# Staging of the cast weights, one bit step on ACT, and a new ranking of all operations in a hashed-attention and channel-mix kernel

## The chip, the core and the metric

The kernel runs on one core of a Trainium2 chip. The metric is the device time of one execution in microseconds. The core has five engines that work side by side: TensorE (PE, matmuls), VectorE (DVE), ScalarE (ACT), GpSimd (POOL), and SyncE (SP), which here only issues DMAs. Each engine takes its instructions in the order in which the program lists them, and an instruction that must wait holds up all that stand behind it on that engine.

## The reference

Attention of 4 batches with 8 heads each, 768 positions and head size 64, in which a query sees only the keys with the same 6 hash bits; its output, laid out as 768 x 512, goes through a channel mix with a squared-ReLU feed-forward and a sigmoid gate.

```
q_bits = (q @ proj > 0);  k_bits = (k @ proj > 0)            # 6 bits each
scores = where(bucket(q) == bucket(k), q @ k.T / 8, -1e9)
attn   = softmax(scores) @ v                                 # 4 x 8 x 768 x 64
x      = attn transposed to 4 x 768 x 512
xk = mu_k * x + (1 - mu_k) * x_prev;  xr = mu_r * x + (1 - mu_r) * x_prev
k  = max(xk @ w_k, 0)                                        # 512 -> 1024
out = sigmoid(xr @ w_r) * ((k * k) @ w_v)                    # 1024 -> 512
```

## The kernel before

The 32 heads are worked in 16 pairs (n = 0 to 15), four pairs to a batch. For a pair, q, k and v are loaded by SP (`nat`, `vn`; 384 KB each). DVE splits q and k into a high and a low fp16 part (`hi` L554 or L614, `lo` L557 or L619), DMA transposes them (`tr`, L561), or, for pairs 0 and 1, PE does (L632) and DVE or ACT copies the result out of PSUM (L637, L639). PE multiplies by the projection (L580, or L656 for pair 0), and DVE turns the signs into two values (`bx`, L583). Four small DMAs of 9 KB (`row`, L593) put these bits as extra rows beside the head dimensions, so that the score matmul (L696) adds a large constant for each bit that agrees; ACT's Exp (L700) with a bias then gives zero wherever a bit differs. For pair 0 the bits are written straight from PSUM, without the DMAs: by DVE (L664), or by ACT with a Sign function (L662). Which engine does which step is in the table `FIRST`, with the three entries split, copy out, bits. PE multiplies by v (L726), DVE divides (L742), the tile is transposed (PE at L752 for the first pairs and the last, else a DMA at L758), and the mixes `xk` and `xr` are formed on DVE. For v itself POOL makes column sums (L511 to L517) from which later pairs subtract the mean (L530, L536).

After four pairs, the batch's channel mix follows: `kp` (L816) with a ReLU on ACT (L820) and a square on DVE (L823) into the twelve tiles `k2`; `r` (L835) with a Tanh on ACT (L838); `v` (L845), and DVE's product (L852) into three tiles `os`, stored by SP. Its matmuls are mixed among those of later pairs' attention.

The weights come as fp32. w_k is converted by the DMA itself, issued from POOL. w_r (two loads, `wl4` and `wl5`) and w_v (four loads, `wl6` to `wl9`) are loaded by SP into an fp32 staging place, 512 KB each (L457), and cast on POOL (`wc4` to `wc9`, L464). Before, the first four stage in the memory of `k2` (L448), which the squares of batch 0 fill later, and the last two in a buffer `wst` of two places (L451).

The order on every engine is made by a planner written in the kernel (`Plan`, L108). Each operation is added with its engine, an assumed duration, what it reads and writes, and a rank. The planner goes through modelled time and lets each free engine take the ready operation with the lowest rank. The ranks are the list `WANT` (L44): its entry i belongs to the i-th operation added (L129). `port=1` marks an operation that the planner lets wait for the port that DVE and POOL share in its model. Loads wait while the modelled DMA queue is over 1.5 us deep (L228), apart from those marked as urgent at the start. The planner runs on the host, when the program is built; the chip sees the resulting order only.

`wl4` to `wc9` are entries 39 to 50 of the list, a load and its cast in turn; entries 51 to 58 are the loads q head 0, q head 1, k head 0, k head 1 and v of pair 0, and q, k and v of pair 1.

Of the kernel before, what the change touches and what calls it, by code (L numbers as in the profile page):

```python
# [9 lines left out]
FP32 = mybir.dt.float32  # L10
# [29 lines left out]
def R(kind, n):  # L40
# [4 lines left out]
    2, 6, 7, 11, 16, 52, 25, 29, 35, 10, 15, 8, 4, 24, 21, 28, 22, 18, 23, 13, 3, 20, 5, 27,  # L45
    14, 1, 32, 34, 36, 39, 40, 19, 51, 37, 48, 61, 76, 88, 102, 320, 346, 409, 435, 478, 500, 382, 412, 366,
    388, 290, 309, 0, 12, 9, 17, 89, 31, 26, 133, 38, 41, 45, 55, 33, 56, 46, 69, 58, 70, 42, 43, 44,
    53, 60, 71, 30, 57, 66, 75, 50, 54, 72, 65, 108, 94, 59, 68, 80, 86, 101, 111, 62, 77, 182, 109, 112,
    116, 123, 49, 78, 99, 92, 73, 63, 87, 98, 74, 64, 96, 85, 47, 67, 84, 93, 107, 95, 124, 115, 119, 113,
    83, 91, 79, 82, 100, 104, 90, 97, 129, 134, 122, 127, 125, 130, 118, 81, 117, 120, 140, 146, 150, 154, 156, 141,  # L50
    155, 159, 163, 165, 168, 172, 175, 177, 185, 180, 110, 103, 240, 148, 152, 158, 161, 106, 105, 126, 121, 114, 138, 162,
    167, 192, 179, 186, 174, 143, 145, 170, 223, 173, 224, 144, 151, 166, 169, 149, 157, 136, 142, 153, 164, 132, 139, 187,
    188, 193, 199, 207, 176, 178, 181, 184, 209, 214, 221, 237, 243, 259, 264, 171, 210, 302, 203, 212, 219, 227, 135, 137,
    147, 128, 131, 160, 183, 190, 215, 202, 226, 206, 233, 235, 230, 232, 249, 250, 211, 222, 218, 217, 200, 204, 197, 195,
    205, 208, 191, 196, 265, 267, 270, 273, 274, 236, 238, 244, 251, 253, 277, 281, 285, 292, 295, 301, 189, 198, 256, 257,
    263, 269, 272, 194, 201, 229, 234, 239, 248, 271, 276, 297, 293, 305, 286, 275, 278, 242, 241, 254, 260, 280, 283, 262,
    314, 282, 288, 245, 246, 258, 266, 225, 216, 289, 291, 294, 300, 306, 296, 298, 299, 307, 312, 317, 322, 325, 327, 331,
    337, 340, 367, 370, 372, 404, 411, 410, 424, 431, 347, 359, 363, 356, 374, 381, 436, 441, 447, 414, 440, 448, 462, 469,
    482, 379, 390, 452, 439, 461, 504, 490, 495, 510, 497, 503, 509, 446, 456, 513, 516, 522, 534, 508, 515, 535, 507, 518,
    531, 467, 472, 520, 547, 551, 586, 473, 480, 539, 556, 561, 609, 532, 555, 571, 583, 591, 619, 599, 608, 559, 587, 615,  # L60
    921, 594, 604, 616, 627, 633, 933, 611, 622, 641, 648, 658, 946, 220, 261, 349, 318, 323, 328, 336, 348, 343, 352, 213,
    228, 279, 231, 247, 268, 303, 308, 324, 316, 330, 345, 339, 351, 361, 377, 329, 338, 354, 360, 321, 332, 334, 344, 315,
    326, 310, 313, 311, 319, 417, 420, 421, 427, 437, 394, 397, 400, 403, 406, 353, 449, 474, 485, 492, 529, 496, 501, 358,
    416, 373, 333, 341, 342, 350, 357, 355, 362, 252, 255, 335, 284, 287, 304, 368, 375, 386, 402, 391, 399, 425, 433, 405,
    418, 376, 383, 401, 413, 384, 393, 387, 398, 457, 465, 392, 407, 364, 369, 451, 454, 455, 464, 499, 481, 487, 494, 512,
    514, 365, 588, 603, 606, 613, 628, 610, 620, 458, 443, 519, 371, 378, 380, 415, 432, 422, 426, 385, 389, 423, 444, 453,
    468, 502, 521, 533, 550, 538, 544, 428, 450, 483, 491, 505, 511, 429, 445, 471, 476, 543, 548, 486, 498, 523, 527, 477,
    484, 526, 528, 530, 537, 540, 552, 567, 577, 582, 593, 430, 602, 632, 634, 645, 649, 647, 652, 395, 489, 541, 396, 408,
    419, 434, 442, 438, 459, 479, 488, 524, 470, 475, 506, 546, 554, 564, 580, 563, 598, 656, 664, 605, 612, 569, 585, 653,
    657, 592, 601, 568, 573, 576, 579, 646, 650, 589, 597, 672, 674, 682, 694, 699, 659, 665, 666, 671, 676, 463, 709, 735,  # L70
    741, 752, 755, 749, 779, 805, 811, 831, 788, 806, 830, 766, 770, 783, 768, 773, 786, 838, 846, 850, 827, 833, 839, 778,
    787, 796, 781, 798, 803, 851, 863, 867, 845, 855, 860, 861, 871, 881, 795, 808, 818, 835, 875, 884, 916, 925, 930, 905,
    911, 915, 910, 918, 926, 815, 826, 931, 939, 942, 961, 880, 886, 923, 943, 949, 958, 902, 951, 948, 959, 963, 966, 978,
    984, 985, 991, 995, 1006, 1005, 1015, 1019, 1029, 1032, 1036, 996, 1004, 954, 974, 1011, 1021, 553, 595, 614, 536, 542, 545, 558,
    566, 572, 581, 460, 466, 493, 517, 525, 574, 635, 640, 654, 651, 663, 678, 661, 670, 683, 693, 679, 686, 607, 617, 621,
    626, 630, 637, 669, 675, 639, 644, 624, 629, 712, 715, 720, 725, 731, 687, 690, 700, 704, 706, 590, 780, 801, 804, 807,
    812, 810, 832, 549, 560, 660, 557, 562, 565, 668, 680, 673, 692, 578, 584, 623, 618, 625, 643, 721, 727, 747, 733, 751,
    739, 705, 714, 696, 702, 710, 719, 703, 707, 726, 728, 732, 742, 740, 748, 729, 734, 717, 723, 737, 743, 750, 756, 784,
    754, 759, 762, 767, 774, 697, 862, 889, 890, 906, 909, 896, 903, 636, 718, 822, 631, 638, 642, 677, 688, 684, 698, 570,
    575, 667, 596, 600, 695, 746, 760, 789, 797, 776, 771, 849, 858, 834, 840, 785, 791, 813, 820, 772, 792, 775, 782, 793,  # L80
    799, 761, 764, 753, 758, 870, 874, 888, 853, 899, 821, 823, 864, 868, 872, 701, 924, 945, 947, 955, 956, 953, 1016, 685,
    745, 852, 681, 689, 691, 708, 722, 713, 730, 655, 662, 724, 738, 744, 763, 800, 825, 856, 844, 837, 847, 857, 865, 895,
    913, 919, 929, 809, 814, 824, 829, 843, 848, 885, 892, 928, 934, 914, 920, 964, 968, 971, 976, 979, 952, 962, 967, 969,
    972, 736, 983, 994, 999, 1003, 1007, 1020, 1022, 1047, 1054, 1058, 1040, 1045, 1051, 1074, 1077, 1085, 1014, 1023, 1026, 1112, 1117, 1122,
    1123, 1126, 1131, 1110, 1116, 1119, 1057, 1065, 1071, 1145, 1151, 1154, 1133, 1140, 1144, 1115, 1124, 1127, 1063, 1076, 1078, 1163, 1169, 1173,
    1147, 1157, 1164, 1177, 1180, 1183, 1101, 1106, 1111, 1082, 1091, 1196, 1197, 1204, 1207, 1167, 1171, 1188, 1193, 1201, 1199, 1209, 1211, 1202,
    1217, 1222, 1227, 1214, 1218, 1148, 1205, 1220, 1223, 1221, 1226, 1236, 1241, 1246, 1249, 1229, 1233, 1224, 1232, 1238, 1242, 757, 794, 869,
    842, 854, 859, 970, 981, 977, 986, 711, 716, 828, 765, 769, 802, 866, 876, 887, 908, 894, 904, 1001, 1008, 993, 998, 1024,
    1027, 891, 897, 957, 960, 941, 944, 901, 907, 877, 882, 1012, 1018, 1031, 1033, 1035, 1038, 1041, 1050, 1052, 1056, 1060, 1064, 987,
    1070, 1087, 1089, 1094, 1100, 1097, 1102, 898, 817, 990, 873, 879, 883, 927, 932, 935, 938, 777, 790, 878, 816, 819, 912, 989,  # L90
    992, 997, 1000, 1010, 1017, 1044, 1048, 965, 980, 1025, 1030, 1061, 1067, 936, 975, 1068, 1073, 1028, 1034, 1107, 1113, 982, 988, 1081,
    1096, 1098, 1105, 1108, 1118, 1121, 1125, 1130, 1134, 940, 1136, 1149, 1150, 1152, 1156, 1159, 1162, 893, 900, 973, 1039, 1043, 1049, 1053,
    917, 922, 950, 836, 841, 937, 1075, 1080, 1099, 1103, 1093, 1086, 1155, 1160, 1104, 1109, 1161, 1165, 1083, 1084, 1037, 1059, 1114, 1120,
    1072, 1079, 1088, 1095, 1092, 1090, 1175, 1176, 1181, 1184, 1185, 1135, 1139, 1158, 1166, 1168, 1055, 1189, 1198, 1200, 1203, 1208, 1206, 1234,
    1002, 1009, 1013, 1042, 1046, 1062, 1066, 1179, 1182, 1170, 1174, 1141, 1146, 1190, 1192, 1129, 1132, 1138, 1142, 1172, 1178, 1128, 1137, 1143,
    1153, 1210, 1212, 1213, 1215, 1216, 1187, 1186, 1191, 1194, 1195, 1069, 1219, 1225, 1228, 1230, 1231, 1235, 1237, 1240, 1239, 1243, 1245, 1258,
    1263, 1265, 1244, 1248, 1251, 1253, 1257, 1259, 1250, 1254, 1256, 1264, 1269, 1271, 1255, 1260, 1262, 1261, 1266, 1268, 1285, 1289, 1291, 1270,
    1275, 1277, 1273, 1278, 1280, 1267, 1272, 1274, 1290, 1295, 1297, 1282, 1286, 1288, 1276, 1281, 1284, 1287, 1292, 1294, 1247, 1252, 1296, 1298,
# [189 lines left out]
def kernel(  # L288
# [52 lines left out]
    def buf(shape, dt, name):  # L341
        return pool.tile(shape, dt, name=name, tag=name)
# [569 lines left out]
```

## Time and profile before

| | us |
|---|---|
| median of 4 runs | 257.84 |
| lowest and highest | 257.11, 258.87 |
| the profiled execution, its own time | 258.16 |
| its span in the profile | 256.4 |
| ACT, the Exps of L700, 144 times | 140.7 |
| PE, scores of L696, 384 times | 82.1 |
| PE, last matmul ends | 252.6 |

The span is the time from the first to the last event of one execution as the profiler saw it; the execution's own time is 1.76 us longer. Busy times of PE overlap a little, because matmuls are pipelined. The granted PE clock is 0.99 in the mean.

### The profile page before, as it was taken

The numbers are of one execution on the slowest core, as the hardware profiler recorded it, in microseconds if no ns is written. First come the engines' busy times: TensorE is split into PE (matmuls) and PEld (weight loads), VectorE is DVE, ScalarE is ACT, GpSimd is POOL, SyncE is SP. The second block draws the span as 40 slices with busy tenths as digits, with TensorE's granted clock in tenths as the row PEclk, the third lists the DMA queues.
The fourth block names the chain that finished last, engine by engine and source line by source line (L and its number), as shares of the span: only waits on it lengthen the run. The fifth ranks groups of instructions, "written<-read, shape, count | busy, mean of one in ns | idle before, by whom it ended". The sixth has DMA issues, their size and how long they took to land.

```text
span 256.4 us, 6170 instructions
## 1 busy us (share of the span) xinstructions
PE 236.7 (92%) x2453; PEld 141.0 (55%) x2453; DVE 188.5 (74%) x416; ACT 181.8 (71%) x241; POOL 50.7 (20%) x89
## 2 busy tenths in 40 slices
PE   8768886987998999999899989999999999999993
PEld 3435654563565655447575655464756674555441
DVE  5998876998686985999799868758665556664322
ACT  4739867849998853799979979466799991347310
POOL 7124350618451123031100053003000000000000
PEclk9999998899999999999999999999999999999998
DMA  6997989969999999899987979974110103220123
GB/s 176 290 257 160 198 254 214 263 195 206 281 293 202 238 230 261 222 272 177 195 219 161 202 179 205 229 212 134 62 31 8 31 3 108 90 82 0 42 83 124
DMA packets 73341, 43.50 MB, mean 170 GB/s; under 512 B 55544, under 2 KB 68192, under 8 KB 73312
## 3 DMA queue, kind: packets, MB, share of 16 engines
q1 hardware_dynamic: 72656, 42.05, 68.0%
q0 software_dynamic: 576, 1.05, 2.2%
q8 instruction: 19, 0.31, 0.5%
q14 instruction: 10, 0.08, 0.1%
q10 hardware_dynamic: 80, 0.00, 0.0%
HBM read 24.12 MB, written 6.29 MB: 119 GB/s over the span
## 4 chain that ended last, share of the span: by engine, by line
PE 58%; DMA 13%; DVE 11%; ACT 7%; SPq 4%; issue 4%; POOL 2%; DVEq 0%; ACTq 0%; POOLq 0%
PE ps_all L845 14%; PE ps_all L696 14%; PE ps_all L816 11%; PE ps_all L726 9%; PE ps_all L835 7%; ACT pt L700 5%; DMA nat<-in_q_dram 4%; PE ps_all L580 2%; SPq L593 2%; DMA mur<-in_moe_mu_r_dram 2%; DMA a<-bx 2%; DMA a<-nh 2%; DVE nh L557 2%; DMA vn<-in_v_dram 2%; DMA nat<-in_k_dram 1%
## 5 line engine op out<-in xcount | busy, mean ns | idle before, releaser
L700 ACT ACTIVATE pt<-ps_all 128x1024 bf16<-128x1024 f32 x144 | 140.7, 1041 | 37.5 <-PE ps_all L696 34.5
L696 PE MATMUL ps_all<-a 128*128 128x512 f16 (+1 forms) x384 | 82.1, 330 | 9.6 <-DMA a<-bx 3.3
L696 PEld LDWEIGHTS <-a 128*128 128x128 f16 x384 | 34.5, 98 | 38.0 <-issue 15.1
L816 PE MATMUL ps_all<-xk,wk 128*128 128x384 bf16 x256 | 48.8, 326 | 0.8 <-ACT kr L820 0.7
L726 PEld LDWEIGHTS <-pt 128*128 128x128 bf16 x1152 | 43.8, 98 | 8.6 <-issue 1.5
L845 PE MATMUL ps_all<-wv,k 128*128 128x512 bf16 x192 | 46.4, 379 | 0.1
L726 PE MATMUL ps_all<-va,pt 128*128 128x65 bf16 x1152 | 46.0, 194 | 0.3 <-ACT pt L700 0.3
L820 ACT ACTIVATE kr<-ps_all 128x384 bf16<-128x384 f32 x64 | 31.4, 508 | 8.5 <-PE ps_all L816 6.1
L823 DVE TENSOR_TENSOR k<-kr 128x384 bf16<-128x384 bf16 x64 | 22.7, 366 | 18.2 <-ACT kr L820 18.1
L816 PEld LDWEIGHTS <-wk 128*128 128x128 bf16 x256 | 24.1, 97 | 16.5 <-issue 1.5
L845 PEld LDWEIGHTS <-k 128*128 128x128 bf16 x192 | 18.2, 98 | 20.4 <-issue 1.0
L838 ACT ACTIVATE rs<-ps_all 128x512 f32<-128x512 f32 x24 | 14.4, 599 | 19.0 <-PE ps_all L835 12.1
L557 DVE SCALAR_TENSOR_TENSOR nh<-nat,nh 128x768 f16<-128x768 f32 x28 | 27.5, 985 | 0.2
L852 DVE SCALAR_TENSOR_TENSOR os<-rs,ps_all 128x512 f32<-128x512 f32 x24 | 16.3, 684 | 14.4 <-PE ps_all L845 12.8
L511 POOL TENSOR_TENSOR vt<-vn 128x384 f32<-128x384 f32 x12 | 12.9, 1074 | 63.4 <-DMA vn<-in_v_dram 63.3
L835 PE MATMUL ps_all<-wr,xr 128*128 128x512 bf16 x96 | 24.3, 379 | 0.3 <-DVE ob L742 0.3
L554 DVE TENSOR_SCALAR nh<-nat 128x768 f16<-128x768 f32 x28 | 16.7, 602 | 9.4 <-DMA nat<-in_q_dram 6.0
L742 DVE TENSOR_TENSOR ob<-ps_all,rc 128x384 bf16<-128x384 f32 x32 | 17.6, 553 | 0.5
L583 DVE TENSOR_SCALAR bx<-ps_all 128x768 uint16<-128x768 uint16 x15 | 14.3, 952 | 3.5 <-PE ps_all L580 2.8
L835 PEld LDWEIGHTS <-xr 128*128 128x128 bf16 x96 | 9.1, 97 | 9.5 <-issue 0.6
L580 PE MATMUL ps_all<-a,p 128*32 128x256 f16 (+1 forms) x240 | 12.9, 329 | 1.6 <-ACT pt L700 0.7
L536 DVE SCALAR_TENSOR_TENSOR va<-ps_all,vn 128x384 bf16<-128x384 f32 x24 | 12.3, 545 | 0.6 <-issue 0.6
(68 smaller groups left out, 160.4 us busy)
## 6 DMA issues: line engine op xcount, KB each, us to landing
vn<-in_v_dram SPq DMA_DIRECT2D x16, 384.0 KB
out_dram<-os SPq DMA_DIRECT2D x24, 256.0 KB
nat<-in_k_dram SPq DMA_DIRECT2D x15, 384.0 KB
nat<-in_q_dram SPq DMA_DIRECT2D x15, 384.0 KB
wk<-in_moe_w_k_dram POOLq DMA_DIRECT2D x4, 256.0 KB, 9.1
wst<-in_moe_w_v_dram SPq DMA_DIRECT2D x2, 512.0 KB
k<-in_moe_w_r_dram SPq DMA_DIRECT2D x2, 512.0 KB
k<-in_moe_w_v_dram SPq DMA_DIRECT2D x2, 512.0 KB
```

What stands on the lines that cost most here:

```text
L554: nc.vector.tensor_scalar(out=nh[:, :, 0:D], in0=nat.rearrange("p j (c d) -> p (j c) d", d=D), scalar1=QS, scalar2=None, op0=ALU.mult)
L557: nc.vector.scalar_tensor_tensor(out=nh[:, :, D:P], in0=nat.rearrange("p j (c d) -> p (j c) d", d=D), scalar=QS, in1=nh[:, :, 0:D], op0=AL ...
L580: nc.tensor.matmul(ps[32 * i : 32 * i + 32, lo:hi], w_, a_t[sa][:, i, lo:hi], start=st, stop=not st)
L696: nc.tensor.matmul(ps[:, lo - s * STEP : hi - s * STEP], side_a["k"][sa][:, j, jc * P : (jc + 1) * P], side_a["q"][sa][:, j, q0 : q0 + hi ...
L700: nc.scalar.activation(out=pt_t[sp][:, s * STEP : (s + 1) * STEP], in_=ps_t[plan.slot[nm]], func=AF.Exp, bias=EBIAS, scale=ESC)
L726: nc.tensor.matmul(oo[:, ic * 65 : ic * 65 + 65], pt_t[sp][:, o : o + P], va_t[sa][:, j, jc, 0 : D + 1], start=(not uc and ic == 0 and jc ...
L742: nc.vector.tensor_tensor(out=ob_t[so][:, :, j * D : (j + 1) * D], in0=oo[:, :, 0:D], in1=rc_t[sr][:, 1, :].unsqueeze(2).to_broadcast([P, ...
L816: nc.tensor.matmul(ps[:, 0:HALF], wk_sb[:, d, fc * P : (fc + 1) * P], xk_t[mx[d]][:, h * HALF : (h + 1) * HALF], start=(d == 0), stop=(d = ...
L820: nc.scalar.activation(out=kr_t[sk], in_=sm(nm)[:, 0:HALF], func=AF.Relu, scale=0.5 ** 0.5)
L823: nc.vector.tensor_tensor(out=k2_t[s2][:, h * HALF : (h + 1) * HALF], in0=kr_t[sk], in1=kr_t[sk], op=ALU.mult)
L835: nc.tensor.matmul(sm(nr), xr_t[mx[d]][:, c * P : (c + 1) * P], wr_sb[:, d, :], start=(d == 0), stop=(d == NDC - 1))
L845: nc.tensor.matmul(sm(nv), k2_t[(b * NFC + fc) % NK2][:, c * P : (c + 1) * P], wv_sb[:, fc, :], start=(fc == 0), stop=(fc == NFC - 1))
```

## The change

Three things change in what is done. The last two weights no longer have `wst` to themselves: `wst` takes the two loads of w_r and, after their casts, the last two of w_v; the first load of w_v stages in the last 2048 columns of `k2`, the second in the first two `os` tiles, which are now slices of one tile. The bits of pair 0's second k head are made by ACT's Sign instead of DVE. And all 1328 ranks in `WANT` are new.

The planner's numbers change with them: casts on POOL count 1.06 instead of 1.1 us, the first v sum of later pairs 1.0 instead of 0.85, and two small DVE steps are marked with `port=1`. A choice to issue some bit rows from ACT is added, with an empty list, and replaces one to issue them from POOL, which was off.

```
 WANT = [
-    2, 6, 7, 11, 16, 52, 25, 29, 35, 10, 15, 8, 4, 24, 21, 28, 22, 18, 23, 13, 3, 20, 5, 27,
-    14, 1, 32, 34, 36, 39, 40, 19, 51, 37, 48, 61, 76, 88, 102, 320, 346, 409, 435, 478, 500, 382, 412, 366,
-    388, 290, 309, 0, 12, 9, 17, 89, 31, 26, 133, 38, 41, 45, 55, 33, 56, 46, 69, 58, 70, 42, 43, 44,
...
+    2, 8, 6, 12, 18, 10, 26, 38, 44, 24, 5, 11, 30, 34, 35, 23, 36, 3, 33, 14, 32, 22, 0, 9,
+    25, 1, 39, 42, 45, 48, 49, 46, 59, 31, 112, 84, 74, 63, 101, 324, 348, 401, 425, 387, 414, 455, 482, 379,
+    403, 446, 470, 4, 41, 13, 37, 102, 21, 7, 117, 47, 50, 52, 51, 65, 66, 53, 19, 58, 40, 54, 17, 68,
...
-    FIRST[(0, "k", 1)] = ("ACT", "ACT", "DVE")
+    FIRST[(0, "k", 1)] = ("ACT", "ACT", "ACT")
...
-    ROW_GQ = False
+    ROW_ACT = ()
...
-    NST = 4
+    WPLACE = (0, 1, "k2", "os", 0, 1)
...
-    os_t = [buf([P, DM], FP32, f"os{i}") for i in range(NOS)]
+    os_all = buf([P, NOS * DM], FP32, "os")
+    os_t = [os_all[:, i * DM : (i + 1) * DM] for i in range(NOS)]
...
-        if z < NST:
-            stage = k2_f[:, z * 2 * DM : (z + 1) * 2 * DM]
-            keys = [("k2", j, h) for j in range(NK2) for h in range(2) if j * S + h * HALF < (z + 1) * 4 * DM and j * S + (h + 1) * HALF > z * 4 * DM]
+        place = WPLACE[z]
+        if place == "k2":
+            top = NK2 * S // 2 - 2 * DM
+            stage = k2_f[:, top:]
+            keys = ["wz"] + [("k2", j, h) for j in range(NK2) for h in range(2) if j * S + (h + 1) * HALF > 2 * top]
+        elif place == "os":
+            stage = os_all[:, 0 : 2 * DM]
+            keys = [("os", 0), ("os", 1)]
         else:
-            stage = wst[:, (z - NST) * 2 * DM : (z - NST + 1) * 2 * DM]
-            keys = [("wst", z)]
+            stage = wst[:, place * 2 * DM : (place + 1) * 2 * DM]
+            keys = [("wst", place)]
...
-        add("POOL", 0.85, pr, f1, r=rk, w=["vt"], port=1, name=f"vsum{n}")
+        add("POOL", 0.85 if uc else 1.0, pr, f1, r=rk, w=["vt"], port=1, name=f"vsum{n}")
...
-            add("DVE", 0.075, R("va", n) + 0.2, fz, r=[("mc", smc)], w=[("xz", sx)], name=f"xz{n}")
+            add("DVE", 0.075, R("va", n) + 0.2, fz, r=[("mc", smc)], w=[("xz", sx)], port=1, name=f"xz{n}")
...
-        add("DVE", 0.12, R("xt", n), fs, r=[("xt", sx)], w=[("xs", sx)], name=f"xs{n}")
+        add("DVE", 0.12, R("xt", n), fs, r=[("xt", sx)], w=[("xs", sx)], port=1, name=f"xs{n}")
```

## The prediction

> **What bounds the kernel now.** I read the page's head and forty-slice table first, then busy time by stages, then the chain of waits, and last the stretches of the timeline where the change acts.
>
> ```profile
> span 256.4 us, 6170 instructions
> ...
> PE 236.7 (92%) x2453; PEld 141.0 (55%) x2453; DVE 188.5 (74%) x416; ACT 181.8 (71%) x241; POOL 50.7 (20%) x89
> ```
> ```profile
> 0.00:18.00 18.00, 13.24 (x101) 7.04 (x102) 14.20 (x31) 8.77 (x13) 5.97 (x32) 1.00 0.93 248
> 18.00:34.00 16.00, 14.14 (x213) 9.44 (x211) 13.28 (x20) 13.03 (x14) 6.42 (x8) 1.00 0.89 181
> 34.00:64.00 30.00, 24.41 (x288) 14.77 (x287) 25.98 (x43) 23.83 (x26) 13.78 (x16) 0.94 0.96 227
> 64.00:180.00 116.00, 112.44 (x1210) 67.47 (x1209) 95.34 (x223) 92.00 (x121) 24.56 (x35) 1.00 0.94 217
> 180.00:252.60 72.60, 72.50 (x649) 42.23 (x646) 39.07 (x102) 44.14 (x68) 0.00 (x0) 1.00 0.15 51
> ```
>
> The columns after the window are its length, then busy us of PE, PEld, DVE, ACT and POOL, the granted clock, the DMA share and GB/s. PE idles 4.76, 1.86, 5.59, 3.56 and 0.10 us in the five stages, and 3.8 us after its last matmul: 19.7 in all. From 64 us on PE is nearly full. So what the change can win lies in the first 64 us (12.2 us of PE idle): whatever brings the start of the full stretch forward ends the kernel earlier, unless later transfers cannot follow. DMA is near its limit to 180 us (share 0.89 to 0.96).
>
> In the opening DVE is the bound. ACT sits idle 3.91 us before its second row below, because the scores of pair 0's second head wait for its bits, and DVE takes three 0.95 us steps in turn: q bits, pair 1's bits, k bits.
>
> ```profile
> 14.65 0.95 DVE L664 TENSOR_SCALAR a<-ps_all 6x768 uint16<-6x768 uint16 x1
> 15.63 0.96 DVE L583 TENSOR_SCALAR bx<-ps_all 128x768 uint16<-128x768 uint16 x1
> 16.62 0.95 DVE L664 TENSOR_SCALAR a<-ps_all 6x768 uint16<-6x768 uint16 x1
> ```
> ```profile
> 13.32 1.02 ACT L700 ACTIVATE pt<-ps_all 128x1024 bf16<-128x1024 f32 x1 [0.69 <-PE ps_all L696]
> 18.26 1.94 ACT L700 ACTIVATE pt<-ps_all 128x1024 bf16<-128x1024 f32 x2 [3.91 <-PE ps_all L696]
> ```
>
> After that SP's queue decides twice: at 28 us, where a load of pair 4 is issued (1.64 us of issue) ahead of pair 2's bit rows, and at 54 us, where pair 4's v comes behind a weight and bit rows.
>
> ```profile
> 28.36 1.64 SPq L485 DMA_DIRECT2D nat<-in_q_dram  x1
> 30.11 1.49 SPq L593 DMA_DIRECT2D a<-bx  x2
> ```
> ```profile
> 52.31 0.44 SPq L457 DMA_DIRECT2D wst<-in_moe_w_v_dram  x1
> 52.80 1.42 SPq L593 DMA_DIRECT2D a<-bx  x2
> 54.27 0.45 SPq L490 DMA_DIRECT2D vn<-in_v_dram  x1
> ```
> ```profile
> 63.39 0.42 POOL vs L517
> ...
> 63.85 0.22 PE ps_all L530
> ```
>
> The last fence is the chain of waits: the v sums of pairs 4 and 5, one after the other on POOL from 58.39 to 63.81, release a matmul for which PE idled 1.02 us.
>
> **What the Trainium skill says.** "DMA: Bandwidth & Descriptors", section "Queues, rings and completion order": SP owns one queue row and each DMA engine consumes descriptors in ring order. So bytes issued earlier delay later ones. The trace agrees in kind: with the queue full, a 9 KB bit row issued at 37.92 released PE only at 43.03. "ScalarE: Activation LUTs", section "Table sets: the hidden batching unit": functions come in sets, and changing the set costs a load. The trace has one table load of 1283 ns at 1.32 us, and both Sign steps (L662) run after it and before the Exps without another, so a Sign between Exps should need none. "SBUF — State Buffer", section "Who interferes with whom": DVE and GpSimd lock a shared port pair. Here the 128x768 step at L557 took 0.92 us alone and 1.55 us at 45.8 with POOL busy. The change tells this only to the planner (two flags and two POOL durations), so it costs nothing itself.
>
> **The change part by part.** Counts of instructions, bytes and DMAs are the same. One L664 of 955 ns leaves DVE; one Sign of 6x768 joins ACT. The trace has Sign at 6x384 (481 ns) and an ACT copy of 128x768 (793 ns); I take 0.80 us, from 0.75 to 0.90. Nothing else than order changes; the list WANT gives each operation a rank, and in the trace before SP issues its opening loads exactly in rank order.
>
> (a) Opening. Gain: k bits on ACT, in the 3.91 us hole, take 0.95 us off DVE. Ranks put pair 1's bits (95 to 110) behind the second head's q bits (94 to 98) and k bits (111 to 103), so the head's scores no longer wait for that 0.96 us either: at best 1.9 us. Against it: SP's first loads become q0, pair 1's k (384 KB), k0, pair 1's q (384 KB), mur, k1, q1 instead of q0, k0, q1, k1. One head is 197 KB, so k0 is complete at 786 instead of 393 KB. Summing the DMA view's half-microsecond slices,
>
> ```profile
> GB/s 0 0 0 58 225 372 227 157 289 216 187 264 313 252 320 321 297 375 359 290 270 238 261 257 245 262 263 258 239 251 259 267 247 294 381 414 255 65 9 18
> ```
>
> 393 KB are in at 3.3 us and 786 KB at 5.05 us: k0 is 1.75 us later, the first Exp about 10.8 instead of 9.07. Four Exps (3.9 us) then end at 14.8, still before the second head, so that is hidden; without that cover it costs 1.75. q1 (1573 KB) is in at about 7.9 plus 0.45 to its reader. Its own chain 0.36+0.56+0.51+0.56+0.81+0.95, with 0.6 for handovers, ends at 12.7; DVE's queue rather than the data still decides. But pair 2's L554, L557, L554 (0.55+0.95+0.55) have ranks 92 to 94, ahead of the q bits, where before one L554 ran: up to 1.5 us more ahead. Restart of ACT: gain from -0.8 (1.5 of fillers, 1.2 of late-data idle on DVE, less 1.9) to +1.9. I take +0.8.
>
> (b) Pair 2. Its first two rows (174, 173) now come before pair 4's loads (182, 192; before 171), and one transpose of pair 2 goes from rank 138 to 114, ahead of pair 1's rows. The 1.64 us issue leaves the way; ACT idled 3.00 us up to 34.29 for these scores. Pair 3's bits (L580), ahead of them on PE, waited for a transpose until 31.91, so part of it comes back as that wait. From 0 to 1.6; I take 1.0.
>
> (c) Pair 4's v. Rank 302 becomes 281, ahead of its bit rows and of pair 5's v (298); the weight at 52.31 (290) moves to 446. The 1.02 us PE wait goes, and POOL's cast of that weight (1.04 us at 56.18) with it. Next late is pair 5's bits, at 65.97. From 0 to 1.0; I take 1.0.
>
> (d) Weights. Six staged weights of 512 KB: before, one is issued at 52.31, four from 58.55 to 71.37, one at 83.03. After, all six lie between ranks 324 and 455. The fifth and sixth use of the own buffer must wait on SP for POOL's casts of the first two. The tight one: wl9 (446) behind wc5 (425). Issue to cast of that load was 71.37 to 77.28, 5.9 us, plus 1.04 for the cast: 6.9. Between them SP issues two rows, two transposes and v of pair 7 (1.4+2.5+2.4+0.4=6.7). The stall is 0.2, from 0 to 2; behind it on SP stand wl7, pair 4's output transpose, q of pairs 8 and 9, pair 8's transposes. I take -0.3. Staging in the output tiles and the last squares adds no live wait: os is first written after all of wv is used, and batch 0's squares now depend on no cast. That release is worth nothing by itself, as PE has 3.56 us idle in 116.
>
> (e) The tail keeps the same set: four or five 0.86 us groups bridge from ot15 to the last MoE, whose PE wait was nil. 0, from -0.5 to +0.5.
>
> Sum: 0.8+1.0+1.0-0.3 = 2.5 us. The profiled execution took 258.16 (span 256.4 and 1.76 around it), giving 255.7; it stands 0.3 above the median 257.84, so 255.3 for the median.
>
> **The rivals.** *More:* the 5 us row wait before 43.03 (PE idle 1.56, clock 0.83 in 40 to 50 us, some 1.4 us of slowed PE) also goes because pair 2 and 3 move ahead: 257.84-2.5-2.5 = 252.8. Against: rows of pair 3 still sit behind three loads and now v as well. *Nothing:* to 180 us the loads are the real bound (share 0.94), PE starts earlier and waits more: 257.8. For: waits for nat at 95 to 142 us in the chain. Against: PE is 97% busy in that stage. *Slower:* weights crowd out pairs 7 and 8. Two more weights (1.05 MB at 247 GB/s, 4.3 us of DMA) fall into 57 to 80 us, where the DMA share already is 1.03, ahead of pair 6's rows and pair 8's q. If all of that reaches PE and half of (a) to (c) survives: +4.3-1.4 = +2.9, 260.7. It decides once PE's idle time between 64 and 100 us grows from about 2.5 by more than the 2.8 won before.
>
> **How the numbers follow.** Forecast 0.50 (own range 253.5 to 256.8), more 0.10, nothing 0.15, slower 0.25. A measurement of this kernel tells about 0.5% (1.3 us) from no change: the limits are 256.55 and 259.13. Faster: 0.50 and 0.10, 0.60; same 0.15; slower 0.25. The range 251.8 to 260.6 takes in the lower bounds of the unknown costs and half of the slower case.
>
> **What would show it.** (a) ACT's first Exp later than 9.07 and its hole before the second head ending near 17.5, no second table load. (b) pair 2's first rows issued right after the transposes, ACT's 3.00 us hole below 2. (c) POOL's sums for pair 4 starting before 56 and no 1.02 us before L530. (d) SP held under 1 us at a weight load. Wrong if the idle time of PE to 64 us stays near 12, or if it rises between 64 and 100.

## The result, and the profile after

| | before | after |
|---|---|---|
| median, us | 256.85 (54 runs) | 254.31 (35 runs) |
| lowest and highest, us | 254.5, 261.16 | 251.25, 259.37 |
| the profiled execution, its own time, us | 258.16 | 253.97 |
| ratio of the times, 95% interval | | 0.9883 [0.9862, 0.9904] |

The kernel is 1.17% faster: 3.0 us of 256.85, or 254.8 on the 257.84 that the forecast of 255.3 started from. The ratio is taken over the fast runs, those within 1.5% of the fastest of their kernel, so it is not the quotient of the two medians, which are of all runs; the profiled executions of three experiments were not among them (the exchange of the two v loads, the splice with the old order behind 34 us, the three moves on SP), and no main reading rests on lengths from these three. The two profiled executions of the table lie 4.2 us apart, because that of before is 1.3 us above its median and that of after close to its own; about 1.2 us of what the two traces show is the draw of the execution and not the change.

The head of the page and the busy time by stages of the kernel after, with the columns as before (length, then busy us of PE, PEld, DVE, ACT, POOL, clock, DMA share, GB/s):

```profile
span 252.2 us, 6171 instructions
...
PE 236.3 (94%) x2453; PEld 140.4 (56%) x2453; DVE 185.6 (74%) x415; ACT 184.0 (73%) x242; POOL 50.3 (20%) x89
```
```profile
0.00:18.00 18.00, 15.01 (x104) 7.12 (x105) 13.26 (x30) 10.17 (x15) 5.58 (x31) 0.91 0.95 257
18.00:34.00 16.00, 12.24 (x184) 8.04 (x182) 11.57 (x18) 13.30 (x14) 7.06 (x8) 1.00 0.79 157
34.00:64.00 30.00, 25.80 (x336) 16.37 (x335) 28.05 (x48) 25.29 (x28) 12.87 (x15) 1.00 0.97 233
64.00:180.00 116.00, 114.92 (x1279) 69.98 (x1276) 95.51 (x231) 94.06 (x123) 24.80 (x35) 1.00 0.93 217
180.00:248.40 68.40, 68.34 (x561) 38.88 (x559) 36.54 (x90) 41.21 (x65) 0.00 (x0) 1.00 0.17 57
```

PE's busy time is the same (236.3 against 236.7), so the gain is idle time of PE. (Each trace has one stage with a lower granted clock, 0.91 to 18 us after and 0.94 from 34 to 64 us before, which lengthens the busy time by up to 1.6 and 1.8 us, an estimate from length and clock of the stage.) The idle time is 2.99, 3.76, 4.20, 1.08 and 0.06 us in the five stages, against 4.76, 1.86, 5.59, 3.56 and 0.10 before. Two things stand out. In the first 34 us, where the forecast put its first term and part of its second, PE idles 6.75 us against 6.62: nothing was won. And from 64 to 180 us, where the forecast put nothing, 2.5 us went.

The opening on ACT and DVE, two views of the timeline of the kernel after. In the bracket is the idle time ahead of the row and what ended it:

```profile
12.45 1.94 ACT L706 ACTIVATE pt<-ps_all 128x1024 bf16<-128x1024 f32 x2
14.42 0.80 ACT L668 ACTIVATE a<-ps_all 6x768 f16<-6x768 f32 x1
15.24 2.05 ACT L706 ACTIVATE pt<-ps_all 128x1024 bf16<-128x1024 f32 x2
17.86 1.94 ACT L706 ACTIVATE pt<-ps_all 128x1024 bf16<-128x1024 f32 x2 [0.57 <-PE ps_all L702]
...
35.51 4.86 ACT L706 ACTIVATE pt<-ps_all 128x1024 bf16<-128x1024 f32 x5 [2.79 <-PE ps_all L702]
```
```profile
14.31 0.95 DVE L563 SCALAR_TENSOR_TENSOR nh<-nat,nh 128x768 f16<-128x768 f32 x1
15.17 0.55 DVE L560 TENSOR_SCALAR nh<-nat 128x768 f16<-128x768 f32 x1
15.64 0.55 DVE L643 COPY a<-ps_all 128x768 f16<-128x768 f16 x1
16.22 0.95 DVE L670 TENSOR_SCALAR a<-ps_all 6x768 uint16<-6x768 uint16 x1
17.91 0.56 DVE L560 TENSOR_SCALAR nh<-nat 128x768 f16<-128x768 f32 x1 [0.73 <-DMA nat<-in_k_dram]
18.38 0.16 DVE L436 TENSOR_SCALAR mur<-mur 128x4 f32<-128x4 f32 x1
18.58 0.96 DVE L589 TENSOR_SCALAR bx<-ps_all 128x768 uint16<-128x768 uint16 x1
```

The Sign stands at 14.42 between Exps and took 0.80 us; no table load stands beside it. The second head's Exps start at 17.86 against 18.26. But the last DVE row, pair 1's bits, starts at 18.58 where before it started at 15.63, and the Exps that had started at 34.29 start at 35.51.

SP at 30, 50 and 76 us (a row is an issue, its length the time that SP spent on it), then POOL's first sum of pair 4 and the matmul that waits for it:

```profile
29.57 0.91 SPq L496 DMA_DIRECT2D vn<-in_v_dram  x1
30.59 1.78 SPq L599 DMA_DIRECT2D a<-bx  x2
...
49.51 0.90 SPq L496 DMA_DIRECT2D vn<-in_v_dram  x1
50.86 1.49 SPq L599 DMA_DIRECT2D a<-bx  x2
52.40 0.44 SPq L496 DMA_DIRECT2D vn<-in_v_dram  x1
...
76.34 0.80 SPq L463 DMA_DIRECT2D wst<-in_moe_w_v_dram  x1
77.19 0.47 SPq L463 DMA_DIRECT2D os<-in_moe_w_v_dram  x1
```
```profile
53.91 1.71 POOL L517 TENSOR_TENSOR vt<-vn 128x384 f32<-128x384 f32 x1 [7.79 <-DMA vn<-in_v_dram]
```
```profile
57.37 0.22 PE L536 MATMUL ps_all<-vs,ones 128*128 128x128 bf16 x1 [0.17 <-POOL vs L523]
```

Pair 4's v is ahead of its bit rows, POOL starts its sums 4.5 us earlier (53.91 against 58.39), and the matmul that had waited 1.02 us waits 0.17.

What PE waited for between 64 and 180 us, from the view of waits (us in total, times, longest), the waits of 0.6 us and more before, then all after (left out is a 1.0 us wait for `vs`, which the view of before lists too but which ended at 63.85):

```profile
PE ps_all L696 <- DVE bx L583: 0.8, 1, 0.8
PE ps_all L580 <- ACT pt L700: 0.7, 1, 0.7
PE ps_all L816 <- ACT kr L820: 0.7, 1, 0.7
PE ps_all L696 <- DMA a<-bx: 0.6, 1, 0.6
```
```profile
PE ps_all L536 <- POOL vs L523: 0.4, 1, 0.4
PE ps_all L851 <- DVE os L858: 0.3, 1, 0.3
```

Four waits of 0.6 us and more, each once and for a different thing, became two shorter ones. The experiments say how much of that is the change: in the profiled executions of two kernels that keep the order of before (the first two below) PE idles only 1.83 and 2.17 us here, and in three that keep the order of after from 48 us on (k bits on DVE, opening loads in the old order, old order to 48 us) 1.64, 1.20 and 0.99. So of the 2.5 us between the two traces about 1 is left.

### The profile page after: what moved, and what is told of

It reads as the page before. It is cut to its first block, busy times and chain, and to the rows that moved or that the text cites. A ratio compares the mean times of both kernels' runs of the same rounds, so it can differ in the third digit from the quotient of the medians.

```text
span 252.2 us, 6171 instructions
## 1 busy us (share of the span) xinstructions
PE 236.3 (94%) x2453; PEld 140.4 (56%) x2453; DVE 185.6 (74%) x415; ACT 184.0 (73%) x242; POOL 50.3 (20%) x89
## 4 chain that ended last, share of the span: by engine, by line
PE 53%; DMA 18%; DVE 11%; SPq 8%; ACT 4%; issue 3%; POOL 1%; DVEq 0%; POOLq 0%
PE ps_all L822 15%; PE ps_all L702 11%; PE ps_all L851 10%; PE ps_all L732 8%; DMA a<-bx 7%; PE ps_all L841 6%; DMA nat<-in_q_dram 4%; SPq L599 4%; DMA nat<-in_k_dram 3%; ACT pt L706 3%; DVE bx L589 3%; PE ps_all L586 2%; DMA vn<-in_v_dram 2%; DMA out_dram<-os 2%; SPq L567 1%
## 5 line engine op out<-in xcount | busy, mean ns | idle before, releaser
L702 PE MATMUL ps_all<-a 128*128 128x512 f16 (+1 forms) x384 | 81.2, 326 | 7.2 <-DMA a<-bx 3.6
L702 PEld LDWEIGHTS <-a 128*128 128x128 f16 x384 | 33.7, 97 | 34.3 <-issue 11.2
L822 PE MATMUL ps_all<-xk,wk 128*128 128x384 bf16 x256 | 47.4, 326 | 0.0
L851 PE MATMUL ps_all<-wv,k 128*128 128x512 bf16 x192 | 47.0, 379 | 0.4 <-DVE os L858 0.3
L826 ACT ACTIVATE kr<-ps_all 128x384 bf16<-128x384 f32 x64 | 30.5, 505 | 7.7 <-PE ps_all L822 4.7
L563 DVE SCALAR_TENSOR_TENSOR nh<-nat,nh 128x768 f16<-128x768 f32 x28 | 28.7, 1034 | 0.3
L560 DVE TENSOR_SCALAR nh<-nat 128x768 f16<-128x768 f32 x28 | 16.1, 575 | 5.6 <-DMA nat<-in_k_dram 2.5
L589 DVE TENSOR_SCALAR bx<-ps_all 128x768 uint16<-128x768 uint16 x15 | 14.3, 955 | 1.6 <-PE ps_all L586 1.1
```

Of the source, the lines that this page charges most:

```text
L563: nc.vector.scalar_tensor_tensor(out=nh[:, :, D:P], in0=nat.rearrange("p j (c d) -> p (j c) d", d=D), scalar=QS, in1=nh[:, :, 0:D], op0=AL ...
L589: nc.vector.tensor_scalar(out=bx_t[sx].bitcast(U16), in0=ps_t[plan.slot[nm]][:, 0:S].bitcast(U16).rearrange("p (c e) -> p c e", e=2)[:, :, 1],
L702: nc.tensor.matmul(ps[:, lo - s * STEP : hi - s * STEP], side_a["k"][sa][:, j, jc * P : (jc + 1) * P], side_a["q"][sa][:, j, q0 : q0 + hi ...
L822: nc.tensor.matmul(ps[:, 0:HALF], wk_sb[:, d, fc * P : (fc + 1) * P], xk_t[mx[d]][:, h * HALF : (h + 1) * HALF], start=(d == 0), stop=(d = ...
L826: nc.scalar.activation(out=kr_t[sk], in_=sm(nm)[:, 0:HALF], func=AF.Relu, scale=0.5 ** 0.5)
L851: nc.tensor.matmul(sm(nv), k2_t[(b * NFC + fc) % NK2][:, c * P : (c + 1) * P], wv_sb[:, fc, :], start=(fc == 0), stop=(fc == NFC - 1))
```

## The experiments

All were timed beside the kernel before; 1% is 2.57 us. The expectations use four theories. A: the opening carries the gain, as steps (a) and (b) had it. B: the opening is decoupled, what it wins is waited away later, and the stage from 34 to 64 us decides. C: the order of the work from 64 us on decides. D, formed after the first traces: the opening after is no better than before, and all is won behind it.

| kernel | ratio to before, 95% interval |
|---|---|
| before + Sign on ACT | 0.9966 [0.9937, 0.9995] |
| before + new staging places | 1.0023 [0.9995, 1.0052] |
| after, k bits on DVE again | 0.9952 [0.9923, 0.9981] |
| after, opening loads in the old order | 1.0020 [0.9989, 1.0050] |
| after, all old ranks, planned anew | 1.0125 [1.0097, 1.0153] |
| after, new ranks to 330, old behind | 1.0023 [0.9997, 1.0049] |
| after, old ranks early, new behind | 1.0090 [1.0055, 1.0125] |
| old order to 34 us, then new | 1.0038 [1.0006, 1.0070] |
| new order to 34 us, then old | 1.0013 [0.9985, 1.0041] |
| old order to 48 us, then new | 0.9892 [0.9845, 0.9939] |
| after, v of pairs 4 and 5 exchanged | 0.9909 [0.9881, 0.9937] |
| before + Sign + three moves on SP | 1.0017 [0.9987, 1.0048] |

**Parts alone, in the old order.** The order is exactly that of before; only the engine of one step, or only the memory of the staging, is another. (In the second, each half of `wst` takes two loads that follow each other, both of w_r or the last two of w_v; in after each half takes one of either.)

```
-                        if e_be == "ACT":
+                        if e_be == "ACT" or (side, j) == ("k", 1):
```

> The kernel before in its own order, with only the k bits of pair 0's second head moved from DVE to ACT. Theory A: 0.95 us off DVE ahead of the second head's Exps goes through to the end: ratio 0.995 to 0.997. Theory B: ACT's hole of 3.91 us shrinks by about 1 us, but the hole of 3.00 us before pair 2 grows by as much, as pair 2's rows hang on SP and DMA: 0.999 to 1.001.

```
-    os_t = [buf([P, DM], FP32, f"os{i}") for i in range(NOS)]
+    os_all = buf([P, NOS * DM], FP32, "os")
+    os_t = [os_all[:, i * DM : (i + 1) * DM] for i in range(NOS)]
...
+        stage = (wst[:, 0 : 2 * DM], wst[:, 0 : 2 * DM], k2_f[:, NK2 * S // 2 - 2 * DM :], os_all[:, 0 : 2 * DM], wst[:, 2 * DM :], wst[:, 2 * DM :])[z]
```

> The kernel before in its own order on every engine, with only the memory of the staged weights moved, to the own buffer, the last squares and the output tiles. All theories: no wait for a cast decided in the trace of before, so 0.998 to 1.002. If the squares did wait for casts without the trace showing it, 0.995 or less.

Sign alone gives 0.34%, 0.9 us, with an interval that almost reaches 1. The timeline of ACT in that kernel shows how little of the freed DVE step comes through at once:

```profile
18.01 10.19 ACT L700 ACTIVATE pt<-ps_all 128x1024 bf16<-128x1024 f32 x11 [2.54 <-PE ps_all L696]
```

The second head starts at 18.01 against 18.26, for 0.95 us taken off DVE. The staging alone gives nothing (its ratio is even 0.2% above 1, with 1 inside the interval). So the earlier release of the first squares of batch 0 pays nothing where the order cannot use it.

**The opening undone, in the new order.** The order of after is kept; in one kernel the k bits go back to DVE, in the other the first loads on SP take the order that they had before.

```
-                        if e_be == "ACT":
+                        if e_be == "ACT" and (side, j) != ("k", 1):
```

> The changed kernel in the same order on every engine, but the k bits of pair 0's second head are made by DVE again, at the place that the Sign had. Theory A (the opening carries the gain, step a of the prediction): DVE gets 0.95 us more ahead of pair 1's bits, which reach the end: 0.7 to 1.2 us slower than the changed kernel, ratio to before 0.991 to 0.993. Theory B (the opening is decoupled by waits for DMA at 23 and 38 us): within 0.4 us of the changed kernel, 0.987 to 0.990.

```
+    at = {o.name: i for i, o in enumerate(order) if o.name}
+    names = ['ldq0q0', 'ldq0k0', 'ldq0q1', 'ldq0k1', 'muk', 'ldq1k', 'ldq1q', 'mur']
+    for i, o in zip(sorted(at[x] for x in names), [order[at[x]] for x in names]):
+        order[i] = o
```

> The changed kernel with its eight opening loads on SP in the order of before (both heads of pair 0 first), all else in the same order. Theory A: the late arrival of k0 is hidden behind DVE's queue: within 0.4 us of the changed kernel (0.987 to 0.990), first Exp near 10 us instead of 12.45. Theory B: DVE and ACT waited for these loads (2.98 and 1.05 us on ACT, 0.43 and 0.33 on DVE), and pair 1's bits come earlier: 0.8 to 1.5 us faster than the changed kernel, 0.983 to 0.985.

Both lose: 0.69% and 1.37% against after, 1.8 and 3.5 us (about 0.9 either way, from the two intervals taken as independent). Undone alone, each takes away more than half of the gain, or all of it. Neither theory expected the second (its first Exp came at 16.29, not near 10), and the first lost more than A had put down. It could still be read as the opening carrying the gain, until the traces are looked at. DVE with the k bits back on it:

```profile
20.65 0.96 DVE L589 TENSOR_SCALAR bx<-ps_all 128x768 uint16<-128x768 uint16 x1
```

and DVE with the old load order, in two stretches:

```profile
8.58 0.63 DVE L620 TENSOR_SCALAR nh<-nat 128x384 f16<-128x384 f32 x2 [4.50 <-DMA nat<-in_k_dram]
...
21.61 0.96 DVE L589 TENSOR_SCALAR bx<-ps_all 128x768 uint16<-128x768 uint16 x1
```

Pair 1's bits, at 18.58 in after, slip to 20.65 and 21.61, by 2.07 and 3.03 us. Pair 2's Exps, which start at 35.51 in after, start 2.07 and 2.82 later, at 37.58 and 38.33 (the first two rows; the third is of the kernel further below in which only the v loads of pairs 4 and 5 are exchanged, near 50 us):

```profile
37.58 11.28 ACT L706 ACTIVATE pt<-ps_all 128x1024 bf16<-128x1024 f32 x12 [2.85 <-PE ps_all L702]
38.33 10.19 ACT L706 ACTIVATE pt<-ps_all 128x1024 bf16<-128x1024 f32 x11 [2.62 <-PE ps_all L702]
37.09 12.02 ACT L706 ACTIVATE pt<-ps_all 128x1024 bf16<-128x1024 f32 x13 [2.60 <-PE ps_all L702]
```

The second case shows how a lag arises: DVE's order still has the k of pair 1 early, its load is now late, and DVE stands 4.50 us with other data lying ready behind (the low part of pair 0's first k head, which before makes at 4.30). The granted clock was lower there too, 0.81 to 18 us against 0.91 in after. The losses, 1.8 and 3.5 us, are of the size of the lags, but that a lag goes through to the end one for one is not shown. The third row has after's opening unchanged and is 1.58 us late as well, so one trace does not fix a lag. And in the traces from which the two lags are read the span is only 1.4 and 1.1 us longer than in after's (253.6 and 253.3 against 252.2). Nor do these runs show that after's opening is ahead of before's, and it isn't: pair 2's Exps start between 35.51 and 37.09 in the three traces with after's opening (this third row and the second splice below are two of them), and between 33.06 and 34.29 in the six with before's.

**Ranks planned anew.** Three kernels are after with other lists of ranks: all of them old; new below 330 and old behind; and the reverse. The planner then makes a new order.

> The changed kernel (staging, Sign on ACT, the planner's new numbers) with the whole list of ranks of before. Theories A and C both put the gain into the ranks: 0.997 to 1.003. If the staging and the Sign carry it, 0.988 to 0.993.

> The changed kernel with the new ranks for the operations whose new rank is below 330 (about the first 60 us), and the ranks of before, behind them, for all others. Theory A (the gain is made in the first 64 us): most of it stays, ratio 0.988 to 0.992. Theory C (the gain is made by the order after 64 us, where PE's idle time fell from 3.56 to 1.08 us): 0.995 to 1.000.

> The reverse: the ranks of before for the operations whose old rank is below 330, the new ranks behind them. Theory A: most of the gain is lost, ratio 0.996 to 1.001. Theory C: most of it stays, 0.988 to 0.993.

All three are slower than after, by 2.4, 1.4 and 2.1%, and the first and the last slower than before, outside every range that was expected for them. They were meant to place the gain in time and can't: the planner builds from such a list an order that neither kernel had, probably because the old ranks were made for other dependences and durations than those of after. In the first, the view of waits (total, times, longest) has PE waiting 3.4 us at one place for pair 0's bits on DVE (1.9 us at the longest before, and none over 0.2 us in after):

```profile
PE ps_all L702 <- DVE a L670: 3.8, 2, 3.4
```

So another list of ranks tests the planner, not the chip. From here on the orders themselves were cut and joined.

**Splices of the two orders.** Everything that the planner placed before 34 us (or 48 us) of its own time is put in one kernel's order, the rest in the other's; everything of after else, except in the second kernel, which has the staging of before with Sign on ACT.

```
+    head = [
...
+    ]
+    plan.slot.update({
...
+    })
+    order = [plan.ops[i] for i in head] + [o for o in order if o.i not in set(head)]
```

> A splice without any new planning: the 203 operations that the kernel before starts up to 34 us of its plan, in its order, then all others in the changed kernel's order; staging and the Sign on ACT as in the changed kernel. Theory A (the opening carries the gain): it is lost, 0.995 to 0.999, as with the Sign alone. Theory D (the opening of the new order is no better or is worse, since its Exp number 19 starts at 35.5 us against 33.3 to 34.3 in three traces of the old order, and the gain is made behind it): all of it stays and the opening's 1 to 2 us come on top, 0.980 to 0.986.

> The reverse splice: the 202 operations that the changed kernel starts up to 34 us of its plan, in its order, then all others in the order of the kernel before, with that kernel's staging; Sign on ACT. Theory A: 0.988 to 0.992. Theory D: slower than before by the opening's 1 to 2 us, 1.002 to 1.008.

> As the first splice, with the cut at 48 us of the plan (282 operations in the old order, before the first weight load and pair 4's v), the rest in the new order. If the gain is made by the order behind 48 us (v of pair 4 ahead, the weight out of the way, MoE of batch 0 among the scores): 0.980 to 0.987. If it is made between 34 and 48 us (no wait of 5 us for pair 3's rows): near the Sign alone, 0.993 to 0.998.

The first is slower than before by 0.38%, outside both ranges expected, and the trace points to the seam. DVE, then PE:

```profile
38.84 0.56 DVE L560 TENSOR_SCALAR nh<-nat 128x768 f16<-128x768 f32 x1 [3.66 <-DMA nat<-in_k_dram]
39.32 0.55 DVE L748 TENSOR_TENSOR ob<-ps_all,rc 128x384 bf16<-128x384 f32 x1
```
```profile
39.93 0.82 PE L758 MATMUL ps_all<-idb,ob 128*128 128x128 bf16 x6 [4.89 <-DVE ob L748]
```

Up to the seam this kernel is ahead of after (the Exps that start at 35.51 there start at 33.4 here). Then DVE stands 3.66 us for the k of pair 4, which at the seam came to be issued behind pair 5's, and PE 4.89 us for the division behind it. Its loss against after, 4.0 us, is about the length of that stall. The second splice gives 1.0013: its interval lies far from what A expected and touches what D expected, but DVE stands 2.15 us for the q of a later pair behind that seam too, so it decides little.

The cut at 48 us has no such seam: from 40 to 64 us DVE waits nowhere longer than 0.79 us. With the old order to 48 us the kernel is as fast as after (0.9892 against 0.9883), although only six runs stand behind it; the ratio lies between the two ranges expected, and its interval reaches into both. Busy time by stages there:

```profile
0.00:18.00 18.00, 14.44 (x106) 7.73 (x107) 13.88 (x31) 10.03 (x15) 6.84 (x32) 1.00 0.92 242
18.00:34.00 16.00, 14.62 (x227) 9.96 (x225) 12.61 (x21) 13.47 (x16) 5.61 (x9) 1.00 1.00 209
34.00:64.00 30.00, 23.27 (x300) 14.63 (x299) 27.30 (x47) 24.84 (x29) 14.06 (x15) 1.00 0.91 217
64.00:180.00 116.00, 115.01 (x1276) 70.19 (x1273) 96.68 (x231) 94.65 (x124) 25.39 (x35) 1.00 0.95 219
```

PE idles 4.94 us to 34 us (6.75 in after) and 6.73 from 34 to 64 (4.20 in after). From 64 to 180 it idles 0.99, as in after. The lead of the old opening, 2.45 us at pair 2's Exps (33.06 against 35.51), is gone by 64 us, as theory B has it: by then ACT has spent 42.6 us on Exps here and 42.5 in after. So no worth of the new opening as a whole is seen against the old one with Sign on ACT (0.2 us, about 1.3 either way), and the rest of the gain is made behind 48 us. That is theory D in where it puts the gain; the 1 to 2 us that D expected from the old opening on top did not come.

**Step (c) alone.** What of the order behind 48 us gains? The forecast named pair 4's v. It was tried from both sides. In after, the loads of v for pairs 4 and 5 were exchanged:

```
+    names = ['ldv5', 'ldv4']
```

> The changed kernel with one exchange on SP: v of pair 5 is loaded where v of pair 4 was, ahead of pair 4's bit rows, and v of pair 4 behind two of them. POOL still sums pair 4 first. Theory A (step c): the 1.02 us wait of PE for the mean comes back: 0.7 to 1.2 us slower than the changed kernel, 0.991 to 0.993. Theory B: PE has other work or waits for Exps there anyway: within 0.4 us of the changed kernel, 0.987 to 0.990.

That costs 0.26%, 0.7 us, less than the intervals separate; the interval reaches into both ranges expected. And before, with Sign on ACT, was given the three moves that step (c) had priced:

```
+    order[at["ldv5"]], order[at["ldv4"]] = order[at["ldv4"]], order[at["ldv5"]]
+    for late, behind in (("wl9", "wl5"), ("wc9", "wc5")):
+        o = order.pop([x.name for x in order].index(late))
+        order.insert([x.name for x in order].index(behind) + 1, o)
```

> The order of before with Sign on ACT, and on SP only three moves: v of pair 4 where v of pair 5 was, v of pair 5 behind the bit rows of pair 4, and weight load wl9 with its POOL cast right behind wl5 and its cast. If step (c) of the prediction carries the gain behind 48 us: POOL's first sum of pair 4 starts before 56 us (58.39 before), PE no longer waits 1.02 us for vs, and the time is about 1.0 us below that of Sign alone, 0.991 to 0.994. Rival: the gain is made by how PE's groups and DVE's pieces are interleaved behind 64 us, and pair 4's v only moves a wait: then as Sign alone, 0.995 to 0.999, with POOL early all the same.

1.0017, where 0.991 to 0.994 was expected, and 0.995 to 0.999 by the rival. The first row below is POOL's first sum of pair 4, the second that of pair 5:

```profile
48.80 1.00 POOL L511 TENSOR_TENSOR vt<-vn 128x384 f32<-128x384 f32 x1
...
56.17 1.00 POOL L511 TENSOR_TENSOR vt<-vn 128x384 f32<-128x384 f32 x1 [5.20 <-DMA vn<-in_v_dram]
```

Both sums start before 58.39, where the first of them stood before, so the moves did what they were to do, and the kernel got no faster than with Sign alone; if anything it is 0.5% slower, though the two intervals just meet. A gain of 1.0 us over Sign alone, 0.991 to 0.994, lies outside the interval. An earlier v is, in the old order, not what pays.

The traces suggest why. The three rows are from the views of PE's waits in the kernel with Sign alone, in that with the new staging places, whose order is the one of before on every engine, and in that with the three moves:

```profile
PE ps_all L816 <- DVE xk L789: 1.3, 1, 1.3
PE ps_all L818 <- DVE xk L791: 0.9, 1, 0.9
PE ps_all L816 <- DVE xk L789: 0.9, 1, 0.9
```

In none of the three does PE wait at the `vs` matmuls of pairs 4 and 5. It waits for `xk` instead, in the first group of `kp`, which follows the first of these matmuls at once (59.01 and 59.09 with Sign alone). In the profile of before it was the other way round: 1.0 us for `vs`, nothing for `xk`. So two inputs are late at one place in the old order, which of them holds PE differs between profiles of that one order, and an earlier v leaves the other. In the new order PE loses at most 0.3 us there (the traces of after, the two with its opening undone and the first and third splice), and more only with the v loads exchanged, where it waits for `vs` again: `kp` starts later, behind score matmuls (61.62 in after, where the first `vs` matmul stands at 57.37). That later `kp` may be one of the moves that pay, of about 1 us; no run tests it alone.

Put together, against before: Sign in the old order 0.9 us [0.1, 1.6]; the new order behind 48 us, with the new staging places, added to that, 0.74% or 1.9 us (about 1.4 either way, from the two intervals taken as independent); the new order ahead of 48 us as well, 0.2 us (about 1.3 either way). Which moves behind 48 us carry the 1.9 us was not settled: single moves out of that order did not bring it. No kernel tried here has a lower ratio than after.

## Why the prediction was right, and where not

The total was right: 2.5 us forecast, 3.0 measured, 255.3 against 254.8. The sum behind it was right in half of its terms at most, so the total is in good part luck: the opening, (a) and (b), was to give 1.8 us and shows no worth beyond that of Sign alone (0.9 us), and about 1 us came from 64 us on, where the forecast had nothing.

**(a), 0.8 us: its premise held, its size did not.** First Exp at 12.45, 3.4 us later than before where 1.7 was forecast, its lateness hidden as forecast; Sign at the estimated 0.80 us; no second table load, so the Sign lies in the set that is loaded for Exp (the Trainium skill, "ScalarE: Activation LUTs", section "Table sets: the hidden batching unit", has a load only at a change of set; the one load in this trace took 1.28 us); the hole before the second head 0.57 us, ending at 17.86, near the 17.5 named. The restart of ACT gained 0.40 us, within the bounds of -0.8 to +1.9. What failed is the step from there to the end: "the head's scores no longer wait for that 0.96 us either: at best 1.9 us" priced who no longer waits and left out who waits instead. Pair 1's bits moved back by 2.95 us: from 14.31 on, a low part, two high parts, a copy, the q bits and a 0.73 us wait for a load stand ahead of them, where before it was the q bits alone from 14.65 on. Their rows moved back with them. At the start of pair 2's Exps the opening was 1.2 us behind in this trace, and 1.2 to 4.0 us over all pairs of traces with the two openings.

**(b), 1.0 us: failed, through (a).** Pair 2's first rows do go out ahead of pair 4's q and k, but at 30.59 against 30.11, and ACT's hole is 2.79 against 3.00, where below 2 was named. The forecast held that SP's 1.64 us issue set the rows' time. In after it is DVE: pair 2's bits (L589) start at 29.41, where before they started at 27.98, because they stand behind a division that waits 2.52 us for PE, which is pair 1's lateness again. Once the bits are later than the load's issue was, taking the load away gains nothing.

**(c), 1.0 us: the mechanism came, its worth was not confirmed.** Every sign named for it appeared (sums before 56, no 1.02 us wait), and PE's idle time from 34 to 64 us fell by 1.4. But the signs do not single it out: with only the staging moved, the first sum stands at 55.46, and neither there nor with Sign alone does PE wait at that matmul. And by itself an earlier v gave no gain in the old order. The steps that failed are "The 1.02 us PE wait goes", put into the sum as 1.0, and "Next late is pair 5's bits, at 65.97": next late, at the same place, was `xk`, at 0.9 to 1.3 us. A wait on the chain of one execution is a bound, and 0 was the other end of the range given.

**(d), -0.3 us: right in kind.** No wait of SP at a weight load: `wl9` was issued in 0.80 us and `wl7` in 0.47, below the 1 us named, and the last weight cast ended at 83.25, earlier than before (87.88). That the staging's release "is worth nothing by itself" is what the run of the staging alone showed.

**The missing term.** "That release is worth nothing by itself, as PE has 3.56 us idle in 116" was taken to mean that the stage from 64 to 180 us could give nothing. Most of its idle time went: 1.08 us is left, about 1 us below what the old order shows in two other kernels. It lay in waits of 0.2 to 0.8 us, each for something else, and the forecast, which went from one long wait to the next, passed over their sum. The rival in which the weights crowd out pairs 7 and 8 fell: PE idles 0.0 us from 64 to 100, where the forecast put the decision at a growth by 2.8. (The "about 2.5" from which it let that growth start is not what the trace of before gives: PE is busy 34.63 of these 36 us, so 1.4.)

## What to carry to other kernels

When a step is put ahead of another on an engine that works in order, price the one that is pushed back, not only the one that is brought forward: here the lag of pair 1's bits stands against two terms of the sum. Before a wait is priced, look in a second trace for what else is late at the same place: here `vs` and `xk` took turns. A stage in which the bounding engine is 97% busy can still hold as much gain, here about 1 us, as the one idle place that the chain of waits points at. And load order and compute order are one design: eight loads exchanged without the compute order gave back all of the gain, and three moves on SP in the old order brought none.

## What the runs showed that was not expected

- Executions of one and the same program on one core scatter by more than the whole effect: 254.5 to 261.16 us before, 251.25 to 259.37 after. A kernel with the order of before and a median of 257.09 was profiled at 252.96. Single traces that differ by 4 us therefore need the ratio of many runs beside them.
- A lead of 2.45 us at pair 2's Exps, in the kernel with the old order to 48 us, was waited away by 64 us: PE's 1.8 us less idle time in the first 34 us came back as 2.5 us more in the next 30.
- Eight loads of unchanged bytes, exchanged in order, left DVE standing 4.50 us and cost 3.5 us in the end: DVE's order had not been changed with them.
